# Spectral mixing and a snake feed-forward: from batch 2 on, one inverse matmul per spectrum class, with the halves of the spectrum swapped by DMA and the product added on VectorE

## The chip, the cores and the metric

The kernel runs on one core of one Trainium2 chip. The metric is the time of one execution in microseconds (us) of the device, taken as the median of several runs. The core has five engines, each working through its own list of instructions in order: TensorE (PE; its weight loads are shown apart as PEld), VectorE (DVE), ScalarE (ACT), GpSimd (POOL) and SyncE (SP). DMAs are issued from an engine's queue and run beside the engines.

## What is computed

The input has 8 batches (the code counts them 0 to 7; the second, number 1, is the first that changes) of 3008 positions and 256 channels.

```
X = rfft(x, axis=1)                    # x: (8, 3008, 256)
y = irfft(X * (filt_r + 1j * filt_i))  # global filter, per channel
h = y @ w_in                           # 256 -> 2048
g = h + sin(alpha * h)**2 / alpha
out = g @ w_out                        # 2048 -> 256
```

## The kernel before, in words

The transform of length 3008 = 47 x 64 is done as matrix products in three stages per batch. **Stage 1** (line 157, tile `pa`) makes 24 classes of the short transform and writes them to DRAM (`d1`). **Stage 2** reads them back with positions on the partitions (`t2`, line 169). For each class, one matmul with the table `d_t` (line 180, `pb`) gives 128 rows: 64 real parts and 64 imaginary parts. ScalarE copies the result of two classes to `xf` (line 183). VectorE multiplies `xf` by the filter's real part and by its imaginary part (line 187, two products `p`), and two accumulated matmuls per class (line 199, `pc`), with the table `e_t` and with a second one whose halves are exchanged and sign-changed, make the complex product and the inverse in one. The result is evacuated to `g` (lines 135 and 137, by ScalarE or VectorE in a rotation of three) and written to DRAM (`d2`, line 206). **Stage 3** loads `d2` as `t4` (line 214) and ends the inverse (line 219, `pd`), into the resident `y`.

The feed-forward part works on 48 chunks of up to 512 columns. For one block of 128 of the 2048 hidden channels, `hidden` does two matmuls (line 356, `ph`), a sine on ScalarE whose phase of pi/2 is read from the tile `quarter` (line 359, `cos`), and one VectorE instruction that forms the snake (line 360, `v`). `project` (line 371, `po`) multiplies the previous chunk's `v` by the second matrix; ScalarE copies the result (line 377) and SP stores it (line 389).

The order of work is a plan by **steps**, eight to a chunk: a step holds two blocks of `hidden` (four `ph` matmuls), whatever pieces of the stages are due, and eight `po` matmuls. `plan` (line 398) gives the due step of each piece of batch b, relative to step 48b: stage 1 at -45 to -38, stage 2 spread from -29 to about -16, stage 3 from -10 on. Batch 1 has its own due steps (line 407). Batch 0 is done ahead of the feed-forward part. A scheduler of the framework then fixes each engine's list and may move an instruction by some places; the pools set how far work may run ahead (PSUM: 4 buffers for `ph`, 2 shared by all stages' matmul results, 2 for `po`; `xf` has 3 buffers, `p` has 4).

The tables and the filter for the upper half of the partitions are made at the start (lines 267 to 292). POOL's queue carries the loads of `x` (line 118), the filters and the weights; SP's queue carries everything else.

Of the kernel before, what the change touches and what calls it, by code (L numbers as in the profile page):

```python
# [9 lines left out]
FP16 = mybir.dt.float16  # L10
FP32 = mybir.dt.float32
AFT = mybir.ActivationFunctionType
# [7 lines left out]
NS, NQ = 24, 64  # L20
NR = 2 * N1
NK = 4 * NS


def dft_tables():
# [29 lines left out]
def kernel(  # L55
# [28 lines left out]
    def pool(name, bufs, space=None):  # L84
        kw = {} if space is None else {"space": space}
        return ctx.enter_context(tc.tile_pool(name=name, bufs=bufs, **kw))
# [3 lines left out]
    t1pool = pool("t1", 4)  # L90
    t2pool = pool("t2", 4)
    xfpool = pool("xf", 3)
    ppool = pool("pp", 4)
    gpool = pool("gp", 4)
    t4pool = pool("t4", 3)
    opool = pool("op", 3)
# [8 lines left out]
    wf_t = cpool.tile([NR, NK], FP16)  # L105
    nc.sync.dma_start(out=wf_t, in_=wf_dram.ap())
    d_t = cpool.tile([128, NS, 128], FP16)
    e_t = cpool.tile([128, 2, NS, 128], FP16)
    wi_t = cpool.tile([NK, NR], FP16)
    f_t = [cpool.tile([128, NS, C], FP16, name=f"filt{i}") for i in range(2)]  # L110

    marks = {}

# [25 lines left out]
    def spectral(b):  # L139
# [8 lines left out]
        def stage1(u):  # L148
# [13 lines left out]
            if u == 7:  # L162
                st["t2"] = []
                for g in range(4):
# [5 lines left out]
                                          in_=d1[a0:a0 + 6, :, :].rearrange("s n c -> n s c"))  # L170
                    st["t2"].append(t2)

        def stage2(u):
            if u < 12:

                ps = (ops if b == 0 else fps).tile([128, 2, C], FP32, name=f"pb_{b}_{u}",
                                                   tag="o" if b == 0 else "f")
                for i in range(2):
                    s = 2 * u + i
                    nc.tensor.matmul(out=ps[:, i, :], lhsT=d_t[:, s, :],  # L180
                                     rhs=st["t2"][s // 6][:, s % 6, :], start=True, stop=True)
                xf = xfpool.tile([128, 2, C], FP16, name=f"xf_{b}_{u}", tag="xf")
                nc.scalar.copy(out=xf, in_=ps)  # L183
                pr = []
                for k in range(2):
                    pt = ppool.tile([128, 2, C], FP16, name=f"p_{b}_{u}_{k}", tag="p")
                    marks["prod", u] = nc.vector.tensor_tensor(out=pt, in0=xf, in1=f_t[k][:, 2 * u:2 * u + 2, :],  # L187
                                                               op=ALU.mult)
                    pr.append(pt)
                st["p", u] = pr  # L190
            if u > 0:
                w = u - 1
                pr = st.pop(("p", w))
                if w % 3 == 0:
                    st["g"] = gpool.tile([128, 6, C], FP16, name=f"g_{b}_{w}", tag="g")
                ps = fps.tile([128, 2, C], FP32, name=f"pc_{b}_{w}", tag="f")
                for i in range(2):
                    for k in range(2):
                        nc.tensor.matmul(out=ps[:, i, :], lhsT=e_t[:, k, 2 * w + i, :],  # L199
                                         rhs=pr[k][:, i, :], start=(k == 0), stop=(k == 1))  # L200
                i0 = 2 * (w % 3)
                evac(st["g"][:, i0:i0 + 2, :], ps, i0 != 2 if b == 0 else None)
                if w % 3 == 2:
                    for p in range(2):
                        a0 = p * NS + 6 * (w // 3)
                        nc.sync.dma_start(out=d2[a0:a0 + 6, :, :].rearrange("s n c -> n s c"),
                                          in_=st["g"][64 * p:64 * p + 64, :, :])

        def stage3(u):
            ch, rest = divmod(u, 4)  # L210
# [13 lines left out]

        for u in range(8):
            pieces.append((1, lambda u=u: stage1(u)))
        for u in range(13):
            pieces.append((2, lambda u=u: stage2(u)))
        for u in range(16):
            pieces.append((3, lambda u=u: stage3(u)))  # L230
        return pieces
# [6 lines left out]
    warm = cpool.tile([128, 1], FP32)  # L238
    nc.vector.memset(warm, 0.0)
    nc.scalar.activation(out=warm, in_=warm, func=AFT.Sin)  # L240
    quarter = cpool.tile([128, 1], FP32)
    nc.vector.memset(quarter, float(np.pi / 2))

    first = spectral(0)
    for _, piece in first[:8]:
# [20 lines left out]

    def dup_filter(g):
        gs = slice(6 * g, 6 * g + 6)
        for k in range(2):
            ins = nc.vector.tensor_copy(out=f_t[k][64:128, gs, :], in_=f_t[k][0:64, gs, :])  # L270
            behind(ins, marks["prod", 3 * g - 2] if g else s1_dve)

    for g in range(4):
        for k, filt in enumerate((filt_r, filt_i)):
            for q in range(2):
                off, step = ((6 * g) * C, C) if q == 0 else ((N1 - 6 * g) * C, -C)
                ins = nc.gpsimd.dma_start(
                    out=f_t[k][32 * q:32 * q + 32, 6 * g:6 * g + 6, :],
                    in_=bass.AP(tensor=filt.tensor, offset=filt.offset + off,
                                ap=[[N1 * C, 32], [step, 6], [1, C]]))  # L280
                if g >= 2:
                    after(ins, marks["t2", g - 2])
    for g in range(3):
        pse = ops.tile([128, 8, 128], FP16, name=f"pse_{g}", tag="o")
        for i in range(8):
            behind(nc.tensor.transpose(out=pse[:, i, :], in_=d_t[:, 8 * g + i, :], identity=id16),
                   s1_pe)
        gs = slice(8 * g, 8 * g + 8)
        behind(nc.scalar.mul(e_t[:, 0, gs, :], pse, 0.125), s1_act)
        nc.vector.tensor_copy(out=e_t[0:64, 1, gs, :], in_=e_t[64:128, 0, gs, :])  # L290
        nc.vector.tensor_scalar(out=e_t[64:128, 1, gs, :], in0=e_t[0:64, 0, gs, :],
                                scalar1=-1.0, scalar2=None, op0=ALU.mult)

    ones = cpool.tile([128, 128], FP32)
    nc.vector.memset(ones, 2.0)
# [53 lines left out]
    def hidden(k, jb):  # L349

        _, c0, n = chunks[k]
        if jb == 0:
            v[k] = vpool.tile([128, 16, 512], FP16, name=f"v_{k}", tag="v")
        ps = hps.tile([128, 512], FP32, name=f"ph_{k}_{jb}", tag="h")
        for cb in range(2):
            nc.tensor.matmul(out=ps[:, 0:n], lhsT=w1[:, cb, jb * 128:jb * 128 + 128],  # L356
                             rhs=y_cols[:, cb, c0:c0 + n], start=(cb == 0), stop=(cb == 1))
        cs = cospool.tile([128, 512], FP32, name=f"cos_{k}_{jb}", tag="c")
        nc.scalar.activation(out=cs[:, 0:n], in_=ps[:, 0:n], func=AFT.Sin, bias=quarter)  # L359
        marks["snake"] = nc.vector.scalar_tensor_tensor(  # L360
            out=v[k][:, jb, 0:n], in0=cs[:, 0:n], scalar=-1.0, in1=ps[:, 0:n],
            op0=ALU.add, op1=ALU.subtract)
# [18 lines left out]
    def store(o_blk, pb, col):  # L381

        p = 0
        while p < 128:
# [11 lines left out]


    plan = {1: [-45 + i for i in range(8)],
            2: [-29 + 14 * i / 13 for i in range(13)],
            3: [-10, -9] + [-7 + 2 * i for i in range(14)]}  # L400
    pending = [(1 + i % 4 + 8 * (i // 4), 0, piece) for i, (_, piece) in enumerate(first[25:])]
    for b in range(1, B):
        at = {1: 0, 2: 0, 3: 0}
        for stage, piece in spectral(b):
            at_step = 48 * b + plan[stage][at[stage]]
            if b == 1 and stage < 3:
                at_step = 8 + at[stage] if stage == 1 else 23 + at[stage]
            at[stage] += 1
            pending.append((at_step, b, piece))
    pending.sort(key=lambda p: p[0])  # L410
# [46 lines left out]
```

## Time and profile before

| what | us |
|---|---|
| median of 3 runs (839.6 to 840.46) | 840.31 |
| the profiled execution: its own time | 841.03 |
| its span, first to last instruction | 839.2 |
| what lies around the span (841.03 - 839.2) | 1.8 |
| TensorE matmuls (PE) busy | 799.2 |
| VectorE (DVE) busy | 628.4 |
| ScalarE (ACT) busy | 674.7 |
| GpSimd (POOL) busy | 28.3 |
| granted TensorE clock, mean over the span | 0.987 of full |

In the views of the profile, a line names an engine, a line of the kernel, the operation and the tiles as out<-in, with buffer numbers left out. The timeline gives the start of a group of equal instructions and how long the group took from the first start to the last end; neighbours on one engine overlap a little, so the pace is read from start to start. "Idle before" is the engine's idle time ahead of a group, with what ended it.

### The profile page before, as it was taken

To read this page: it belongs to the slowest core of one execution; us is meant where nothing else is said; L and a number is where in the kernel's file an instruction comes from. 1 tells how busy PE (TensorE), PEld (TensorE's weight loads), DVE (VectorE), ACT (ScalarE), POOL (GpSimd) and SP (SyncE) were. 2 spreads that over 40 slices of the span, in tenths; PEclk is the share of its full clock that TensorE was granted. 3 is DMA by queue.
4 is the path that set the end of the run, shared out by engine and by line. 5 is a ranking of instruction groups with operands and counts; after the bars stand their busy time and mean duration, and the time that the engine had idled before them with its cause. 6 is when DMAs were issued, how large, how long until landed. Compare 5 with 4: busy or idle time off the path is not lost.

```text
span 839.2 us, 16120 instructions
## 1 busy us (share of the span) xinstructions
PE 799.2 (95%) x5793; PEld 544.1 (65%) x5793; DVE 628.4 (75%) x1120; ACT 674.7 (80%) x1200; POOL 28.3 (3%) x55
## 2 busy tenths in 40 slices
PE   6748999999999999999999999999999999999996
PEld 2324676667776676666776677666767677666674
DVE  3658786777877787777877788777877778777772
ACT  4546897888878898888888888888988988788873
POOL 3210000000000000000000000000000000000000
PEclk9978999999999999999999999999999999999999
DMA  9985845184344734367242763447343343421111
GB/s 216 219 252 116 190 98 130 48 182 106 88 133 82 181 86 98 88 128 167 66 126 61 168 136 81 117 87 171 91 97 94 98 113 82 115 57 38 38 39 45
DMA packets 93495, 94.98 MB, mean 113 GB/s; under 512 B 8084, under 2 KB 82852, under 8 KB 93416
## 3 DMA queue, kind: packets, MB, share of 16 engines
q1 hardware_dynamic: 84784, 75.02, 34.4%
q0 software_dynamic: 6704, 18.09, 12.4%
q10 hardware_dynamic: 1928, 0.86, 0.5%
q8 instruction: 45, 0.74, 0.4%
q14 instruction: 34, 0.28, 0.1%
HBM read 58.02 MB, written 49.81 MB: 128 GB/s over the span
## 4 chain that ended last, share of the span: by engine, by line
PE 82%; DMA 7%; DVE 4%; ACT 4%; issue 2%; SPq 0%; POOL 0%; ACTq 0%; DVEq 0%; POOLq 0%
PE ph L356 35%; PE po L371 35%; PE pc L199 5%; PE pa L157 4%; PE pd L219 2%; DMA t<-d 2%; PE pb L180 2%; ACT cos L359 2%; DMA d<-t 1%; DMA w_out<-in_moe_w_out_dram 1%; DVE v L360 1%; DVE p L187 1%; DMA d<-g 1%; ACT t L135 1%; DMA filt<-in_filt_r_dram 1%
## 5 line engine op out<-in xcount | busy, mean ns | idle before, releaser
L360 DVE SCALAR_TENSOR_TENSOR v<-cos,ph 128x512 f16<-128x512 f32 (+1 forms) x768 | 483.8, 671 | 148.1 <-ACT cos L359 147.1
L359 ACT ACTIVATE cos<-ph,quarter 128x512 f32<-128x512 f32 (+1 forms) x768 | 480.6, 680 | 103.9 <-PE ph L356 101.6
L371 PE MATMUL po<-w,v 128*128 128x256 f16 x3008 | 401.3, 273 | 4.2 <-DVE w L339 4.2
L356 PE MATMUL ph<-y,w 128*128 128x512 f16 (+1 forms) x1536 | 391.3, 376 | 0.3 <-ACT y L135 0.2
L371 PEld LDWEIGHTS <-v 128*128 128x128 f16 x3008 | 289.0, 98 | 80.7 <-issue 8.9
L356 PEld LDWEIGHTS <-w 128*128 128x128 f16 x1536 | 150.6, 98 | 102.8 <-issue 5.5
L187 DVE TENSOR_TENSOR p<-xf,filt 128x512 f16<-128x512 f16 x192 | 72.1, 418 | 6.2 <-ACT xf L183 5.4
L377 ACT COPY o<-po 128x512 f32<-128x512 f32 x96 | 56.5, 589 | 9.8 <-PE po L371 7.4
L183 ACT CAST xf<-pb 128x512 f16<-128x512 f32 x96 | 56.6, 591 | 8.8 <-DMA t<-d 5.7
L135 ACT CAST t<-pa 96x512 f16<-96x512 f32 x89 | 50.0, 588 | 16.4 <-PE pa L157 16.4
L199 PE MATMUL pc<-p,e_t 128*128 128x256 f16 x384 | 59.9, 276 | 2.9 <-DVE p L187 1.5
L219 PEld LDWEIGHTS <-t 96*128 96x128 f16 x512 | 35.5, 98 | 39.0 <-DMA t<-d 11.8
L157 PE MATMUL pa<-x,wf_t 94*96 94x512 f16 x128 | 47.6, 410 | 9.7 <-DMA x<-in_x_dram 5.8
L219 PE MATMUL pd<-wi_t,t 96*128 96x94 f16 x512 | 42.3, 207 | 11.1 <-DMA t<-d 10.6
L135 ACT CAST y<-pd 128x376 f16<-128x376 f32 x82 | 38.7, 474 | 12.2 <-PE pd L219 12.2
L199 PEld LDWEIGHTS <-e_t 128*128 128x128 f16 x384 | 37.7, 99 | 15.7 <-issue 7.5
L180 PE MATMUL pb<-t,d_t 128*128 128x256 f16 x192 | 38.2, 283 | 3.5 <-DMA t<-d 2.4
L135 ACT CAST g<-pc 128x512 f16<-128x512 f32 x64 | 38.7, 605 | 2.2 <-PE pc L199 1.9
L137 DVE CAST y<-pd 128x376 f16<-128x376 f32 x46 | 25.2, 548 | 19.3 <-PE pd L219 19.1
L137 DVE CAST t<-pa 96x512 f16<-96x512 f32 x39 | 26.7, 684 | 16.8 <-PE pa L157 16.1
L180 PEld LDWEIGHTS <-d_t 128*128 128x128 f16 x192 | 18.7, 101 | 25.4 <-DMA t<-d 4.5
L118 POOL DMA_DIRECT2D x<-in_x_dram x32 | 16.6, 522 | 504.6 <-PE pa L157 494.0
(29 smaller groups left out, 86.1 us busy)
## 6 DMA issues: line engine op xcount, KB each, us to landing
d<-t SPq DMA_DIRECT2D x32, 384.0 KB
d<-g SPq DMA_DIRECT2D x64, 192.0 KB
t<-d SPq DMA_DIRECT2D x32, 384.0 KB
x<-in_x_dram POOLq DMA_DIRECT2D x32, 376.0 KB, 7.2
t<-d SPq DMA_DIRECT2D x60, 192.0 KB
out_dram<-o SPq DMA_DIRECT2D x72, 94.0 KB
w_in<-in_moe_w_in_dram POOLq DMA_DIRECT2D x2, 1024.0 KB, 9.0
w_out<-in_moe_w_out_dram POOLq DMA_DIRECT2D x1, 2048.0 KB, 12.4
```

What stands on the lines that cost most here:

```text
L135: marks["act"] = nc.scalar.copy(out=dst, in_=src)
L157: marks["pe"] = nc.tensor.matmul(out=ps[0:NK, :], lhsT=wf_t, rhs=st["x"][ch][:, n0:n0 + 2, :], start=True, stop=True)
L180: nc.tensor.matmul(out=ps[:, i, :], lhsT=d_t[:, s, :], rhs=st["t2"][s // 6][:, s % 6, :], start=True, stop=True)
L183: nc.scalar.copy(out=xf, in_=ps)
L187: marks["prod", u] = nc.vector.tensor_tensor(out=pt, in0=xf, in1=f_t[k][:, 2 * u:2 * u + 2, :], op=ALU.mult)
L199: nc.tensor.matmul(out=ps[:, i, :], lhsT=e_t[:, k, 2 * w + i, :], rhs=pr[k][:, i, :], start=(k == 0), stop=(k == 1))
L219: nc.tensor.matmul(out=psv[:, i, :], lhsT=st["t4"][:, 4 * half + i, cb * 128:cb * 128 + 128], rhs=wi_t, start=True, stop=True)
L356: nc.tensor.matmul(out=ps[:, 0:n], lhsT=w1[:, cb, jb * 128:jb * 128 + 128], rhs=y_cols[:, cb, c0:c0 + n], start=(cb == 0), stop=(cb == 1))
L359: nc.scalar.activation(out=cs[:, 0:n], in_=ps[:, 0:n], func=AFT.Sin, bias=quarter)
L360: marks["snake"] = nc.vector.scalar_tensor_tensor(out=v[k][:, jb, 0:n], in0=cs[:, 0:n], scalar=-1.0, in1=ps[:, 0:n], op0=ALU.add, op1=ALU. ...
L371: nc.tensor.matmul(out=pso[k][:, t % 2, :], lhsT=v[k][:, jb, 128 * t:128 * t + 128], rhs=w2[:, jb, :], start=(jb == 0), stop=(jb == 15))
L377: nc.scalar.copy(out=o[:, 0:nb, :], in_=pso[k][:, 0:nb, :])
```

## The change

Batch 0 keeps the old form (`stage2_first`), with the second table in three tiles of the pool `t4`. From batch 1 in the code's count, which is the second batch, a pair of classes u is worked on so:

- The forward matmuls and the copy to `xf` are as before. Two DMAs on POOL's queue, each of 64 partitions by 1 KB (64 KB), copy the lower half of `xf` to the upper half of a new tile `xs` and the upper half to the lower.
- VectorE multiplies `xf` by the filter's real part at once. Three steps later (`SWAP = 3`) it multiplies `xs` in place by the imaginary part, whose lower half now holds the negated values, and adds it to the first product: three VectorE instructions per pair where there were two.
- One step after that, one inverse matmul per class with `e_t` makes the result: two `pc` matmuls per pair where there were four.
- Stage 2 has 16 pieces in place of 13, at one per step from -30 to -15; for batch 1, from step 23 to 37 (before: 23 to 35).
- The sine takes its phase of pi/2 as a number in the instruction and not from a tile.

```diff
+SWAP = 3
-    ppool = pool("pp", 4)
+    ppool = pool("pp", 7)
+    xspool = pool("xs", 5)
...
         def stage2(u):
+
             if u < 12:
...
+                xf = forward(u)
+                xs = xspool.tile([128, 2, C], FP16, name=f"xs_{b}_{u}", tag="xs")
+                for p in range(2):
+                    nc.gpsimd.dma_start(out=xs[64 * p:64 * p + 64, :, :],
+                                        in_=xf[64 - 64 * p:128 - 64 * p, :, :])
+                st["p", u] = product(u, 0, xf), xs
+            w = u - SWAP
+            if 0 <= w < 12:
+                pt, xs = st["p", w]
+                nc.vector.tensor_tensor(out=xs, in0=xs, in1=f_t[1][:, 2 * w:2 * w + 2, :], op=ALU.mult)
+                nc.vector.tensor_tensor(out=pt, in0=pt, in1=xs, op=ALU.add)
+            w = u - SWAP - 1
+            if w >= 0:
+                inverse(w, [st.pop(("p", w))[0]])
...
-        for u in range(13):
-            pieces.append((2, lambda u=u: stage2(u)))
+        for u in range(13 if b == 0 else 13 + SWAP):
+            pieces.append((2, lambda u=u: (stage2_first if b == 0 else stage2)(u)))
...
-        nc.scalar.activation(out=cs[:, 0:n], in_=ps[:, 0:n], func=AFT.Sin, bias=quarter)
+        nc.scalar.activation(out=cs[:, 0:n], in_=ps[:, 0:n], func=AFT.Sin, bias=float(np.pi / 2))
...
-            2: [-29 + 14 * i / 13 for i in range(13)],
+            2: [-30 + i for i in range(13 + SWAP)],
...
-                at_step = 8 + at[stage] if stage == 1 else 23 + at[stage]
+                at_step = 8 + at[stage] if stage == 1 else 23 + 14 * at[stage] / 15
```

`forward`, `product` and `inverse` are the old lines of `stage2` cut into functions; `inverse` does one matmul per class for each product that it is given. At the start, the imaginary filter is loaded to the upper half of the partitions and its negated copy made for the lower half, and the second table of batch 0 is made by two sign changes in place of a copy and a sign change.

## The prediction

> **What bounds the kernel now.** First the page's busy times, then the slices, then the chain.
>
> ```profile
> PE 799.2 (95%) x5793; PEld 544.1 (65%) x5793; DVE 628.4 (75%) x1120; ACT 674.7 (80%) x1200; POOL 28.3 (3%) x55
> ...
> PE   6748999999999999999999999999999999999996
> ...
> PE 82%; DMA 7%; DVE 4%; ACT 4%; issue 2%; SPq 0%; POOL 0%; ACTq 0%; DVEq 0%; POOLq 0%
> ```
>
> TensorE is full from the fourth slice to the last but one, and the chain runs over it for 82% of the span. So the worth of a removed matmul is its own pace, as long as nothing else fills the hole. The windows view says what else is there: stage 2 of batch 3, and the stretch up to stage 2 of batch 4 (columns: us, then the busy time of PE, PEld, DVE, ACT, POOL).
>
> ```profile
> 291.31:327.82 36.51, 36.29 (x270) 25.96 (x268) 30.89 (x61) 31.77 (x57) 0.00 (x0) 1.00 0.40 90
> 327.82:390.10 62.28, 62.10 (x463) 41.94 (x461) 46.65 (x75) 52.47 (x94) 2.05 (x4) 1.00 0.55 129
> ```
>
> In stage 2 TensorE is busy for 36.29 of 36.51, but VectorE and ScalarE for some 31: only 5 to 6 us of cover each. The timeline gives the paces there.
>
> ```profile
> 301.86 0.75 DVE L187 TENSOR_TENSOR p<-xf,filt 128x512 f16<-128x512 f16 x2
> 302.53 0.68 DVE L137 CAST g<-pc 128x512 f16<-128x512 f32 x1
> 303.13 1.27 DVE L360 SCALAR_TENSOR_TENSOR v<-cos,ph 128x512 f16<-128x512 f32 x2
> 304.32 0.75 DVE L187 TENSOR_TENSOR p<-xf,filt 128x512 f16<-128x512 f16 x2
> ...
> 319.78 0.31 PEld L180 LDWEIGHTS <-d_t 128*128 128x128 f16 x2
> 320.00 0.38 PE L180 MATMUL pb<-t,d_t 128*128 128x256 f16 x2
> 320.22 0.60 PE L199 MATMUL pc<-p,e_t 128*128 128x256 f16 x4
> 320.65 1.04 PE L371 MATMUL po<-w,v 128*128 128x256 f16 x8
> 321.53 1.03 PE L356 MATMUL ph<-y,w 128*128 128x512 f16 x4
> ```
>
> From start to start: two `pb` 0.22, four `pc` 0.43, eight `po` 0.88, so 0.108 us per 256-column matmul. VectorE: two products 0.67 (0.335 each), a `g` evacuation 0.60, two snakes 1.19 (0.595 each). A plain step, `ph` and `po` alone, takes 1.74 (327.83 to 329.56 in the same timeline).
>
> **The removed matmuls.** Two per pair, 12 pairs, 7 batches: 168 x 0.108 = 18.1 us of TensorE. Their weight loads (99 ns in the group of line 199) lie under the matmuls and free nothing.
>
> **What VectorE then does to it.** I take the 17 steps from 291.31 to 329.56 of batch 3, 38.25 us. TensorE's work in them is 17 x 1.74 + 24 `pb` (2.6) + 48 `pc` (5.2) + one `pd` piece (0.17) = 37.5; 0.7 are short waits, mostly when VectorE does a `g`. After: 34.9. VectorE's own work rises from 34 x 0.595 + 24 x 0.335 + 4 x 0.60 = 30.7 to 34.7 (36 products and sums). So the two engines tie, and the load is uneven. By the built program's list for batch 3, eleven steps, from the fourth pair's on, hold 22 snakes, 28 products and sums and 4 evacuations: 13.1 + 9.4 + 2.4 = 24.9 us for VectorE, against 11 x 1.74 + 8 x 0.217 + 10 x 0.217 = 23.0 for TensorE. VectorE falls behind by 1.9. How much of that TensorE feels: a step's `ph` needs the snakes of two steps earlier (4 buffers), which leaves about 2 us, but an inverse matmul waits for its sum, and by the list it stands only 0.4 to 1 us behind it; behind the waiting `pc` stand all `po` and `ph`. I take 1.0 as absorbed, 0.9 as lost, and 0.3 of short waits kept: 34.9 + 0.9 + 0.3 = 36.1, a gain of 2.1 per batch. The ends are all lost (1.2) and nothing lost (3.3).
>
> **The swaps.** 168 DMAs of 64 KB on POOL's queue; the trace has none like them. The `x` loads stand ahead of the swaps in POOL's list, but wait only for stage 1 of the batch before, which is done 10 steps earlier, so they don't block. An `x` load on that queue occupies POOL for 0.51 us, moves its first packet 1.2 us after the start (at 264.5, 362.7, 557.5), and lands 0.3 after its last. With 4 packets per DMA engine at 0.05 to 0.07 us (the 1 KB stores), two swaps take 0.1 + 0.5 + 1.2 + 0.6 + 0.3 = 2.7 us from `xf` to landing, an estimate from these rows. The nearest whole rows are longer: filter loads of 96 KB at 27.7 to 31.6 took 4.6 to 5.4, the first of them with 2.9 us to its first packet beside `t2` loads; the `x` loads 4.6 to 8.3. I take 2.9, since outside the `t2` loads the DMA engines are 27 to 36% busy here, and keep 2.0 and 5.4 as the ends. VectorE's wait for a swap is in its list: behind it stand the snakes, and behind those ScalarE and `ph`. The plan leaves three steps (some 6 us), but the list puts the product of pair 0 in the very next step, and pair 3's too: about 2.7 us after `xf`. So 2.9 costs 0.2 to 0.4 once per batch, and the first pairs meet the tail of the `t2` loads, which run until 294.2 to 296.0 in batches 3 and 4 and to 492.3 in batch 5 (6.7 us into the window). I charge 0.5 per batch in all. At 5.4 it would be 2.5 more, at 2.0 nothing.
>
> The Trainium skill, DMA: Bandwidth & Descriptors, section "Anatomy of one DMA — SWDGE (gpsimd) path", gives about 2.0 us plus bytes/436e3 for such a DMA: 2.15 us for one swap, and 2.7 for two that start 0.5 apart. By that the first product would be on time and the 0.5 would be the `t2` tail alone.
>
> POOL's issues may be slower beside the products: the filter loads' at 27.7 to 31.6, among batch 0's products, took 0.49 to 0.78 us, at most 0.3 longer than the 0.51, which the three steps cover and the two early products pay at 0.3 each at worst.
>
> The Trainium skill, SBUF — State Buffer, section "SBUF: two separate sides", has a warning against this very queue: descriptors made by GpSimd are held up while VectorE runs in a two-port mode; the section "Who interferes with whom" takes products of two tensors out of that. By the warning every swap would come late, as in rival C; by the exception none.
>
> **Stage 3's start.** Stage 2 ends later: in the list the last `pc` stands two steps further on, with only 7.9 to 8.8 us of `po` and `ph` between it and the first `pd` (10.4 before). The chain in batch 3 was: `pc` ends 325.38, evacuated 326.34, two stores issued until 327.87, their packets end 331.1, `t4` issued 331.53, its packets end 334.1. That is 8.8. So 0 to 0.9 missing, 0.45 each, in batches 2 to 7: 2.7 us. In batch 1 the wait shows already:
>
> ```profile
> 143.43 0.33 SPq L214 DMA_DIRECT2D t<-d  x1
> 144.25 0.36 PEld L219 LDWEIGHTS <-t 96*128 96x128 f16 x8 [1.79 <-DMA t<-d]
> 144.26 0.51 PE L219 MATMUL pd<-wi_t,t 96*128 96x94 f16 x8 [1.51 <-DMA t<-d]
> ```
>
> There the chain took 10.75 (133.51 to 144.26). The list now fills it with 72 `po` (7.8 us), the whole of chunk 4's, and so has few left to mix into chunk 5, where TensorE will run at the pace of ScalarE and VectorE. I charge 1.5 more at the wait and 1.0 in chunk 5: 2.5, between 0 and 6.
>
> **The phase as a number.** `cos` takes 690 ns for 128x512, the same-sized copy of line 377 597 ns. Between 0 and 93 ns off 768 instructions, at most 71 us of ScalarE, which is not the bound: its cover is TensorE. It keeps ScalarE (busy 31.77 of 36.5 in stage 2) from becoming the bound in the shorter steps, and is worth up to 2 us where chunks 0 and 1 wait for it; I take 0.5. Cost elsewhere: none; the start-up's filter and table edits replace VectorE instructions one for one.
>
> **Sum.** 7 x (2.1 - 0.5) = 11.2; less 2.7, less 2.5, plus 0.5: 6.5 us off 841.03, so 834.5 by the profiled execution. The median shown is 0.7 lower; I forecast **834.0**.
>
> **Rivals.** (A) TensorE keeps all: VectorE's lag is absorbed and the swaps land in time. 7 x 3.3 = 23 less some 3 at stage 3: 820. For it, the 2 us of room at `ph`; against it, the tie of 34.9 and 34.7. Chance 0.12. (B) Gains and losses cancel within 0.2% (838.6 to 842.0): `pc` waits for its sum each time and all of the lag is lost, 7 x (1.2 - 0.5) - 2.7 - 2.5 + 0.5 = 0.2, so 840.1. For it, the sums that stand 0.4 us ahead of their `pc`; against it, the 2 us at `ph`. Chance 0.14. (C) Slower: swaps that land late. Each us beyond 2.9 delays VectorE once per batch at pair 0, by the list, and since VectorE has no idle time left the delay goes through to `pc`: 7 us per us. The 6.5 are used up at 3.8, and from 4.1 on it is slower by over 0.2%; at 5.4 it is 834 + 17.5 = 851.5. For it, the filter loads' 4.6 to 5.4; against it, that these read from DRAM beside full DMA engines. Chance 0.20. (D) That the change does not do what it says can be left out for the matmuls (the list has two per pair), and for the phase it would give back 0.5 and slow the lag's recovery; inside the range.
>
> The forecast's own case, 824 to 838.6, has 0.54. Faster by over 0.2% (about what a measurement of this kernel can tell from no change) is then 0.66, same 0.14, slower 0.20. The range, 820 to 848, leaves out about 0.2.
>
> **What would show it.** Line 199's successor with 216 matmuls; VectorE near 95% busy in the 17 steps and these 36 to 37 us long; two landings of a swap about 0.5 apart, the later some 2.9 us after its `xf`; waits of `pc` for the sum, short ones of the `xs` product for a DMA, and `pd` for `t4` of about 0.5 per batch and some 3 in batch 1; `cos` near 600 ns. Wrong it would be if the swaps took over 4 us, or if the 17 steps took over 38.

## The result, and the profile after

The change made the kernel slower: 862.11 us median (858.54 to 866.68, 4 runs) beside 840.38 for the kernel before in the same comparison, a ratio of 1.026 (1.020 to 1.031). The profiled execution took 860.53, with a span of 858.7 us and a granted clock of 0.983 (before: 0.987).

In the changed kernel's lines, `pb` is L186, `xf` L189, the first product L194, `pc` L204, the `d2` stores L211, the swaps L228, the product of the swapped half L234, the sum L235, the `t4` loads L245, `pd` L250, `ph` L388, `cos` L391, `v` L392, `po` L403 and the out stores L421. The page of the changed kernel: busy times, TensorE's slices, and the chain.

```profile
PE 787.1 (92%) x5625; PEld 523.7 (61%) x5625; DVE 650.5 (76%) x1203; ACT 617.1 (72%) x1200; POOL 115.8 (13%) x223
...
PE   6749988998999988999899989899899999899996
...
PE 64%; DMA 16%; DVE 8%; ACT 5%; issue 4%; SPq 1%; POOL 1%; ACTq 0%; DVEq 0%; POOLq 0%
```

The matmuls are gone as planned (5793 to 5625, 168 fewer), and TensorE is busy for 12 us less. But its row of nines now has eights all through, and the chain runs over DMAs for 16% of the span where it had 7%. TensorE lost more to waiting than it gained. The view of waits names the two new ones (us in total, times, longest).

```profile
PE pd L250 <- DMA t<-d: 23.4, 8, 8.6
...
DVE xs L234 <- DMA xs<-xf: 21.0, 10, 3.2
```

Before, `pd` waited for `t4` 10.6 us in 2 waits, 9.1 of them in batch 0; now it waits in every batch, 8.6 us in batch 0 and 14.8 in the other seven. The wait of VectorE for a swap is new: 21.0 us over 10 waits, one or two in each of seven batches.

To place the loss, I cut both spans at the first `ph` of a step, and measure the 17 steps that hold stage 2, the 8 steps after them up to the `pd` pieces, and the rest of each batch.

| stretch, us | before | after | difference |
|---|---|---|---|
| start to step 22 | 101.0 | 99.3 | -1.8 |
| batch 1: stage 2, 17 steps | 38.4 | 38.3 | -0.1 |
| batch 1: start of stage 3, 3 steps | 8.0 | 14.4 | +6.4 |
| batch 1: the 23 steps behind that | 45.9 | 41.1 | -4.8 |
| batches 2 to 7: stage 2, 17 steps each | 230.4 | 233.8 | +3.4 |
| batches 2 to 7: the 8 steps up to `pd` | 85.6 | 101.7 | +16.0 |
| batches 2 to 7: rest | 329.9 | 330.1 | +0.3 |
| span | 839.2 | 858.7 | +19.5 |

So there are two losses. Stage 2, which has 24 matmuls fewer in each batch, became no shorter. And the start of stage 3 costs 16 us more.

**Loss one, at the head of stage 2.** The timeline of batch 3 (start, duration, engine, what; in brackets the idle time before, with what ended it).

```profile
294.35 0.59 ACT L189 CAST xf<-pb 128x512 f16<-128x512 f32 x1
...
295.23 1.06 POOL L228 DMA_DIRECT2D xs<-xf  x2 [15.22 <-ACT xf L189]
...
300.48 0.42 DVE L234 TENSOR_TENSOR xs<-xs,filt 128x512 f16<-128x512 f16 x1 [2.75 <-DMA xs<-xf]
...
302.02 1.19 PE L388 MATMUL ph<-y,w 128*128 128x512 f16 x4 [1.11 <-DVE v L392]
...
302.64 1.19 ACT L391 ACTIVATE cos<-ph 128x512 f32<-128x512 f32 x2 [1.54 <-PE ph L388]
```

`xf` is done at 294.94 and POOL starts 0.29 us later, but the swapped halves are there only at 300.45, 5.5 us after `xf`. VectorE stands 2.75 us, the snakes queued behind it are late, and TensorE's `ph` waits for them. A second, later wait of TensorE (1.61 us, `pc` at 309.8) belongs to the same disturbance: in experiments 1 and 2 no such wait is left. From `xf` to both halves landed, pair 0 took 5.6, 5.6, 5.5, 5.1, 6.3, 4.3 and 5.0 us in batches 1 to 7; pairs 4 and 5, with few packets of SP's queue beside them, took mostly 2.6 to 3.3.

**Loss two, at the start of stage 3.** The timeline of batch 3 in the kernel before: SP's queue and `pd`.

```profile
326.61 1.26 SPq L206 DMA_DIRECT2D d<-g  x2
331.53 0.32 SPq L214 DMA_DIRECT2D t<-d  x1
332.11 1.89 SPq L389 DMA_DIRECT2D out_dram<-o  x5
334.04 0.78 SPq L214 DMA_DIRECT2D t<-d  x2
335.64 0.33 PE L219 MATMUL pd<-wi_t,t 96*128 96x94 f16 x4
```

The same in the changed kernel.

```profile
331.55 1.97 SPq L211 DMA_DIRECT2D d<-g  x2
...
333.83 2.16 SPq L421 DMA_DIRECT2D out_dram<-o  x5
...
336.46 1.25 SPq L245 DMA_DIRECT2D t<-d  x3
...
342.47 0.81 PE L250 MATMUL pd<-wi_t,t 96*128 96x94 f16 x8 [3.10 <-DMA t<-d]
...
344.56 1.06 PE L388 MATMUL ph<-y,w 128*128 128x512 f16 x2
```

Before, the first `t4` load was issued alone, and five out stores and the other two loads behind it. Now five out stores go ahead of it, and three loads are issued back to back. `pd` comes 6.0 us after the first load's issue; before, it came after 4.1 and did not wait. Besides, stage 2 ends nearer to `pd`: between the end of the last `pc` and `pd`, TensorE has 7.9 to 8.8 us of other work (the cover) in batches 2 to 7 (10.3 before), while the chain of evacuation, stores and load takes 9.1 to 11.9.

In this batch the wait of 3.10 us cost 5.0. The windows view shows why (columns as in the prediction; the clock is the third from the end).

```profile
339.40:342.40 3.00, 0.00 (x0) 0.00 (x0) 1.28 (x2) 0.54 (x2) 0.00 (x0) 0.97 0.90 255
342.40:344.00 1.60, 1.53 (x13) 1.29 (x14) 0.55 (x1) 0.47 (x1) 0.00 (x0) 0.50 0.10 38
344.00:346.00 2.00, 2.00 (x10) 1.12 (x9) 0.00 (x0) 0.58 (x1) 0.00 (x0) 0.60 0.00 0
346.00:348.00 2.00, 2.00 (x18) 1.28 (x16) 1.11 (x2) 1.63 (x4) 0.00 (x0) 1.00 0.37 107
```

With the wait TensorE's granted clock fell to half for 3.4 us, and its matmuls took twice as long: some 1.7 us on top.

### The profile page after: what moved, and what is told of

It reads as the page before. It is cut to its first block, busy times and chain, and to the rows that moved or that the text cites. A ratio compares the mean times of both kernels' runs of the same rounds, so it can differ in the third digit from the quotient of the medians.

```text
span 858.7 us, 16160 instructions
## 1 busy us (share of the span) xinstructions
PE 787.1 (92%) x5625; PEld 523.7 (61%) x5625; DVE 650.5 (76%) x1203; ACT 617.1 (72%) x1200; POOL 115.8 (13%) x223
## 4 chain that ended last, share of the span: by engine, by line
PE 64%; DMA 16%; DVE 8%; ACT 5%; issue 4%; SPq 1%; POOL 1%; ACTq 0%; DVEq 0%; POOLq 0%
PE ph L388 28%; PE po L403 28%; DMA t<-d 6%; DMA xs<-xf 5%; PE pa L164 3%; DVE v L392 3%; PE pc L204 2%; DMA d<-g 2%; PE pd L250 2%; ACT cos L391 2%; DMA d<-t 2%; DVE p L194 2%; DMA w_out<-in_moe_w_out_dram 1%; ACT t L142 1%; DVE xs L234 1%
## 5 line engine op out<-in xcount | busy, mean ns | idle before, releaser
L392 DVE SCALAR_TENSOR_TENSOR v<-cos,ph 128x512 f16<-128x512 f32 (+1 forms) x768 | 485.1, 671 | 133.9 <-ACT cos L391 133.2
L391 ACT ACTIVATE cos<-ph 128x512 f32<-128x512 f32 (+1 forms) x768 | 415.8, 591 | 141.0 <-PE ph L388 138.1
L403 PE MATMUL po<-w,v 128*128 128x256 f16 x3008 | 405.9, 273 | 2.5 <-DVE w L371 2.5
L388 PE MATMUL ph<-y,w 128*128 128x512 f16 (+1 forms) x1536 | 397.8, 377 | 7.7 <-DVE v L392 7.0
L403 PEld LDWEIGHTS <-v 128*128 128x128 f16 x3008 | 290.0, 98 | 82.4 <-issue 8.7
L388 PEld LDWEIGHTS <-w 128*128 128x128 f16 x1536 | 150.2, 98 | 106.7 <-issue 15.2
L228 POOL DMA_DIRECT2D xs<-xf x168 | 87.2, 524 | 270.5 <-ACT xf L189 266.4
L250 PEld LDWEIGHTS <-t 96*128 96x128 f16 x512 | 35.8, 101 | 52.8 <-DMA t<-d 26.7
L189 ACT CAST xf<-pb 128x512 f16<-128x512 f32 x96 | 57.4, 599 | 11.9 <-DMA t<-d 5.1
L250 PE MATMUL pd<-wi_t,t 96*128 96x94 f16 x512 | 43.5, 210 | 24.0 <-DMA t<-d 23.4
L142 ACT CAST t<-pa 96x512 f16<-96x512 f32 x89 | 51.1, 589 | 18.8 <-PE pa L164 18.7
L204 PE MATMUL pc<-p,e_t 128*128 128x256 f16 x192 | 39.9, 280 | 14.3 <-DVE g L144 8.5
L234 DVE TENSOR_TENSOR xs<-xs,filt 128x512 f16<-128x512 f16 x84 | 34.5, 419 | 21.0 <-DMA xs<-xf 21.0
L194 DVE TENSOR_TENSOR p<-xf,filt 128x512 f16<-128x512 f16 x108 | 43.9, 419 | 5.7 <-ACT xf L189 5.4
L142 ACT CAST g<-pc 128x512 f16<-128x512 f32 x64 | 38.0, 593 | 12.0 <-PE pc L204 11.2
L186 PE MATMUL pb<-t,d_t 128*128 128x256 f16 x192 | 37.8, 280 | 3.7 <-DMA t<-d 2.8
L204 PEld LDWEIGHTS <-e_t 128*128 128x128 f16 x192 | 14.6, 99 | 34.3 <-DVE p L235 16.4
```

The lines of the kernel that those rows point to most:

```text
L142: marks["act"] = nc.scalar.copy(out=dst, in_=src)
L194: marks["prod", u] = nc.vector.tensor_tensor(out=pt, in0=x, in1=f_t[k][:, 2 * u:2 * u + 2, :], op=ALU.mult)
L204: nc.tensor.matmul(out=ps[:, i, :], lhsT=e_of(k, 2 * w + i), rhs=pt[:, i, :], start=(k == 0), stop=(k == len(pr) - 1))
L228: nc.gpsimd.dma_start(out=xs[64 * p:64 * p + 64, :, :], in_=xf[64 - 64 * p:128 - 64 * p, :, :])
L250: nc.tensor.matmul(out=psv[:, i, :], lhsT=st["t4"][:, 4 * half + i, cb * 128:cb * 128 + 128], rhs=wi_t, start=True, stop=True)
L392: marks["snake"] = nc.vector.scalar_tensor_tensor(out=v[k][:, jb, 0:n], in0=cs[:, 0:n], scalar=-1.0, in1=ps[:, 0:n], op0=ALU.add, op1=ALU. ...
```

## The experiments

**1. No swaps.** The product reads `xf` itself; there are enough `xf` buffers, and `xs` is made by the product.

```diff
-                for p in range(2):
-                    nc.gpsimd.dma_start(out=xs[64 * p:64 * p + 64, :, :],
-                                        in_=xf[64 - 64 * p:128 - 64 * p, :, :])
...
-                nc.vector.tensor_tensor(out=xs, in0=xs, in1=f_t[1][...], op=ALU.mult)
+                nc.vector.tensor_tensor(out=xs, in0=xf_w, in1=f_t[1][...], op=ALU.mult)
```

> The changed kernel without its 168 swap DMAs: the product with the imaginary part reads the unswapped spectrum itself, so the exchange of the halves is left out of what is computed. Instructions on TensorE, VectorE and ScalarE are as many as in the changed kernel. Theory (late swaps): VectorE's idle 2 to 3 us ahead of the first such product of a batch goes, the 17 steps of stage 2 fall from a mean of 39.0 us by about 2 to 36.5 to 37.3, and seven batches give 13 to 16 us: 846 to 849 where the changed kernel takes 862. The start of stage 3 stays as long as it is (16 us over batches 2 to 7 more than before the change). Rival (VectorE bound by its 84 further instructions): the 17 steps stay at 38 to 39, and the time stays over 857. Rival (the swaps' traffic is what makes stage 3 late): the eight steps up to the first pd shrink by 2 to 3 us per batch as well, and the time is below 840.

Measured: 841.39 (838.12 to 844.09, 10 runs), ratio to the kernel before 0.999 (0.996 to 1.001). The 17 steps have a mean of 35.8 us over batches 2 to 7 (changed kernel 39.0, before 38.4), VectorE has no idle time ahead of these products, and the eight steps up to `pd` stay long: 100.7 in all (101.7 in the changed kernel). It came out below the 846 to 849 expected, since the 17 steps fell by 3.2 where I had put 2. VectorE's 84 further instructions do not hold the stage up, and the swaps' traffic is not what makes stage 3 late. Both rivals fall.

**2. The product where the plan means it.** `behind` puts an instruction behind another one in its engine's list.

```diff
+                if u < 12:
+                    behind(ins, marks["prod", u])   # ins: the product of xs of pair w = u - 3
```

> The changed kernel, with the product of pair u's swapped spectrum put behind the first product of pair u+3 in VectorE's list, three steps later, where the plan means it to be; the swaps are as before. Theory (late swaps met too early by VectorE's list): no idle time of VectorE ahead of these products is left, though the swaps still take 4 to 6 us; the 17 steps fall to 36.5 to 37.5 us and the time to 847 to 852. Rival (VectorE bound by its further instructions): the 17 steps stay at 38 to 39 and the time within 4 us of 862. Rival (the sum now stands too close ahead of its inverse matmul): the wait moves from VectorE to pc, the 17 steps get no shorter.

Measured: 845.28 (840.21 to 850.53, 10 runs), ratio 1.005 (1.003 to 1.008). The swaps take as long as before (pair 0: 4.5 to 6.0 us), but nobody waits. The same place in batch 3 of this kernel:

```profile
292.95 1.07 POOL L228 DMA_DIRECT2D xs<-xf  x2 [15.22 <-ACT xf L189]
...
299.40 0.42 DVE L234 TENSOR_TENSOR xs<-xs,filt 128x512 f16<-128x512 f16 x1
...
300.34 0.39 PE L204 MATMUL pc<-p,e_t 128*128 128x256 f16 x2 [0.20 <-DVE p L237]
```

And the 17 steps of batch 3 (us, then PE, PEld, DVE, ACT, POOL), first of the changed kernel:

```profile
290.84:329.33 38.49, 35.76 (x261) 24.30 (x259) 34.76 (x74) 30.07 (x59) 12.45 (x24) 1.00 0.61 137
```

then of this one:

```profile
288.56:324.20 35.64, 35.36 (x258) 23.86 (x256) 33.83 (x72) 30.12 (x59) 12.46 (x24) 1.00 0.64 146
```

TensorE is busy for 35.36 of 35.64 us and VectorE for 33.83: the tie holds without loss. The mean of the 17 steps is 35.8, as without swaps. So loss one was the place of the product in VectorE's list together with the swaps' 4 to 6 us, and it is worth 3.2 us per batch. What is left against the kernel before is stage 3's start (+18.7 in batches 2 to 7).

**3. The first `t4` load apart from the second.** `after` makes an instruction wait for the end of another one, here for the landing of the first load.

```diff
+                if b > 0 and ch == 1:
+                    after(ins, marks["t4"])   # ins: the second t4 load
```

> The changed kernel, with the second t4 load of each batch from batch 1 on issued only when the first has landed, so that the first has the DMA engines to itself; the engines' lists are the same. Theory (three loads issued back to back share the engines, so the first lands in 6 us and not in 2.6): it lands in about 3 us, the wait of pd falls by 2 to 3 us in each of batches 2 to 7, and the time falls by 10 to 16 us to 846 to 852. Rival (the chain is long because stage 2 ends later, whatever the loads do): the first load's time falls, but the time stays within 3 us of 862, or the wait moves to the second load's matmuls four steps later.

Measured: 856.86 (855.94 to 860.79, 4 runs), ratio 1.019 (1.016 to 1.022). The median is some 5 us below the changed kernel's where 10 to 16 were expected, and the spreads of the two overlap; the eight steps up to `pd` fell from 101.7 to 98.5. From the first load's issue to a `pd` that waits for it, it takes 3.6, 3.5 and 4.6 us in batches 2, 4 and 6 (4.2, 4.6, 5.4 in the changed kernel), and 5.4, 5.1 and 4.4 in batches 3, 5 and 7 (6.0, 5.9, 6.4), which have five out stores right ahead of it and not four. So the loads that follow it are one part of what slows the first. That the stores ahead of it are the other is not shown by this run, in which batch 7 with five of them took less than batch 6 with four.

**4. Stage 3 three steps later, in the even batches.**

```diff
+            if stage == 3 and b % 2 == 0:
+                at_step += 3
```

> The changed kernel, with stage 3 of batches 2, 4 and 6 due three steps later; the odd batches as they were, since their y is needed sooner, so they are the contrast inside the kernel. Theory (the start of stage 3 is a chain of 10 to 12 us that is no longer covered): in batches 2, 4 and 6 the wait of pd goes, and with it the 1.5 to 2.5 us that each of them loses in the eight steps up to pd; in all 4 to 6 us, 856 to 858, and nothing in batches 3, 5 and 7. Rival (work is only moved: TensorE or VectorE is short of time there anyway): the time stays within 2 us of 862, since what is gained at pd is lost where the pd pieces now stand closer together.

Measured: 863.56 (859.29 to 865.92, 4 runs), ratio 1.025 (1.022 to 1.029). The first half held: in batches 2, 4 and 6 the wait of `pd` is gone, and the eight steps take 13.9 us each (15.6 to 16.3 in the changed kernel). But the 17 steps of stage 2 in batches 2, 3 and 5 grew by 1.9, 2.5 and 0.8, the eight steps of batch 5 by 2.0, and the time did not fall. Part of this is the clock: the granted clock was at half for 3.4 us in batch 2's 17 steps (mean 0.96) and in batch 5's eight (mean 0.91), which costs 1.7 us each, and in neither of the two in the changed kernel (mean 1.00). In batches 3, 5 and 7, `pb` waits 1.7, 1.4 and 1.4 us for a `t2` load (1.0 in batch 5 of the changed kernel, and no such wait in 3 and 7); the `pd` pieces of the batch before, now later, may be what delays these loads, which no run shows. The time is the rival's, but only a part of the gain at `pd` was moved to other places; the clock took another part.

**5. The first `t4` load ahead of the out stores** (from experiment 2). It is issued with the last `d2` stores, and the out stores are put behind it in SP's list.

```diff
+            if b > 0 and w == 11:
+                load_t4(0)          # at the end of inverse(11)
...
+            behind(ins, marks["t4"])    # ins: an out store
```

> The kernel with the late product (845.28), and with the first t4 load of each batch put right behind the last d2 stores in SP's list, ahead of the out stores that now stand between them and ahead of the other t4 loads. Theory (the first load shares the DMA engines with four or five out stores and two further t4 loads, and so lands in some 6 us where it took 2.6): it lands in about 3 us, pd finds it about 8 us after the last pc, where the cover is 7.6 to 7.8 us by the list, the waits of 1.5 to 3.3 us fall under 0.6, and the time is 829 to 835. Rival (only the shrunken cover counts): the load gets shorter by less than 1 us, and the time stays over 840.

Measured: 830.83 (828.55 to 834.18, 4 runs), ratio 0.987 (0.984 to 0.990). Batch 3:

```profile
323.13 1.76 SPq L211 DMA_DIRECT2D d<-g  x2
327.19 0.32 SPq L218 DMA_DIRECT2D t<-d  x1
327.61 1.99 SPq L427 DMA_DIRECT2D out_dram<-o  x5
329.65 0.32 SPq L218 DMA_DIRECT2D t<-d  x1
330.76 0.34 PE L256 MATMUL pd<-wi_t,t 96*128 96x94 f16 x4 [0.67 <-DMA t<-d]
```

From issue to `pd` 3.3 to 3.7 us in all batches, and waits of 0.1 to 1.3. The cover is even shorter here than in the changed kernel (7.6 to 7.9 us), and still the eight steps come down from 104.3 to 90.9 us. Of these 13.4, about 10.5 are waits of `pd` (13.6 in experiment 2, 3.1 here), and 3.4 are the clock, which was at half for 3.4 us in batches 3 and 5 of experiment 2 and nowhere in these steps here. So most of loss two was the order of SP's list.

**6. Stages 1 and 2 three steps earlier** (from experiment 2).

```diff
-    plan = {1: [-45 + i for i in range(8)],
-            2: [-30 + i for i in range(13 + SWAP)],
+    plan = {1: [-48 + i for i in range(8)],
+            2: [-33 + i for i in range(13 + SWAP)],
```

> The kernel with the late product (845.28), with stages 1 and 2 of batches 2 to 7 due three steps earlier, so that 10.9 to 11.4 us of po and ph stand between the last pc and the first pd by TensorE's list where it had 7.9 to 8.6. Theory (the start of stage 3 is the rest of the loss, and is a matter of cover): with a chain of 9.5 to 11.8 us the waits fall from 1.5 to 3.3 us to under 0.9, the eight steps up to pd come back to 14 to 15 us from 15.8 to 19.3, and the time is 827 to 833. Rival (the work is only moved and collides with stage 3 of the batch before): the rest of each batch grows by what pd gains, and the time stays within 4 us of 845.

Measured: 828.33 (826.69 to 829.16, 4 runs), ratio 0.983 (0.982 to 0.985). The eight steps take 85.3 us, as before the change (85.6), and no `pd` waits from batch 2 on. The rest of the batches grew by 2.7, since stage 2 now begins two steps ahead of the 17, so little of the gain is given back. TensorE now has 10.7 to 11.2 us of other work between the last `pc` and `pd`. So more cover alone cures loss two as well.

**7. All three together:** the late product, the early load and the earlier plan.

> Late product, first t4 load ahead of the out stores, and stages 1 and 2 three steps earlier, all together. Theory: a chain of about 8 us under a cover of 10.9 to 11.4, so no wait for t4 from batch 2 on; what is left against the kernel before is batch 1's wait of about 2 us. 826 to 830. If it is no faster than the better of the two parts, either part alone was enough to cover the chain. Rival (SP's list, held up by the early load, delays the out stores and through the three o buffers the copies on ScalarE): waits of the o copy for out stores, and a time over 832.

Measured: 827.10 (826.57 to 828.53, 4 runs), ratio 0.982 (0.981 to 0.984): this version beats both kernels, by 1.8% and 4.1%. It is within the spread of experiment 6, so the earlier plan is enough, and the early load adds nothing clear to it. The 17 steps of batch 3 and the eight behind them:

```profile
286.62:322.21 35.59, 35.48 (x258) 23.77 (x256) 35.32 (x75) 30.33 (x58) 11.41 (x22) 1.00 0.50 124
322.21:336.79 14.58, 14.57 (x110) 9.88 (x108) 10.71 (x18) 10.20 (x20) 0.00 (x0) 1.00 0.49 140
```

TensorE and VectorE are both full in stage 2, and TensorE behind it: in stage 2, the matmuls that the change took away are now time that is saved.

**8. The swaps from SP's queue** (the changed kernel, early product).

```diff
-                    nc.gpsimd.dma_start(out=xs[64 * p:64 * p + 64, :, :],
+                    nc.sync.dma_start(out=xs[64 * p:64 * p + 64, :, :],
```

> The changed kernel, with the swaps issued from SP's queue in place of POOL's; product and plan as in the changed kernel. Theory A (the swaps are slow because their queue's packets get small turns beside the other queue's loads): on the other queue two swaps land 2.5 to 3.5 us after xf, VectorE's wait at pair 0 falls under 1 us, and the time falls by 8 to 13 us to 849 to 854. Theory B (the DMA engines are busy with the t2 loads, whatever the queue): they land after 4 to 6 us as before, and the time stays within 4 us of 862. Rival C (in SP's list the swaps stand behind stores and loads that wait): swaps begin late, the first over 1 us after xf, and the time is over 866.

Measured: 863.26 (859.52 to 869.00, 4 runs), ratio 1.025 (1.019 to 1.030). The time is theory B's, but in batches 1 to 6 the first swap starts 1.8 to 3.7 us after `xf`, as rival C has it, and VectorE still waits 17.3 us. Two things were changed at once, the queue and the place of the swaps behind SP's loads and stores, so the time tells nothing of the queue. But from its issue to the product that waited for it, pair 0's swap took 3.5 to 5.8 us here, and 4.0 to 6.0 from issue to landing on POOL's queue: the other queue did not make it quick, and theory A falls.

**9. Stage 1 four steps earlier** (the changed kernel), so that the `t2` loads are done before the first swaps.

```diff
-    plan = {1: [-45 + i for i in range(8)],
+    plan = {1: [-49 + i for i in range(8)],
```

> The changed kernel, with stage 1 of batches 2 to 7 due four steps (some 7 us) earlier and nothing else moved: VectorE's list for stage 2 is the same, with the early products, but the t2 loads are done before the first swaps start. Theory (the first swaps take 4 to 6 us because they share the DMA engines with the tail of the t2 loads): pair 0's swaps land 2.6 to 3.5 us after xf, VectorE's wait ahead of the first product falls from 1.6 to 3.2 us to under 0.8, the 17 steps from 39.0 to about 37, and the time to 848 to 853. Rival (these swaps are slow by themselves on POOL's queue): they still land after 4 to 6 us, and the time stays within 4 us of 862.

Measured: 863.98 (862.03 to 866.17, 4 runs), ratio 1.027 (1.025 to 1.030). My theory of the `t2` tail falls in this form. Pair 0's swaps did shorten, to 3.1 to 3.9 us in batches 2, 4, 6 and 7, with waits under 1 us; in batches 3 and 5 they still took 5.1. And where pair 0 was in time, VectorE waited for pair 1 or 2 in its place (2.6, 1.7, 2.4, 0.9 us in batches 2, 4, 6, 7). In all, VectorE waited 17.3 us where it had waited 21.0. Something else slows them: in the trace, out stores lie around these swaps.

**10 and 11. The out stores around the first swaps left out**, with stage 1 as in experiment 9 and then with stage 1 as the change has it.

```diff
+        if step > 48 and (step + 31) % 48 < 8:
+            return                  # in store()
```

> Stage 1 of batches 2 to 7 four steps earlier (as in the kernel that took 863.98), and the out stores of the eight steps around the first swaps of each of these batches left out, so that a part of the output is not written. Theory (a swap is slow whenever packets of SP's queue, of either kind, share the DMA engines with it): with neither t2 loads nor out stores beside them, the swaps of pairs 0 to 2 land 2.6 to 3.2 us after xf in every one of these batches, VectorE waits less than 0.5 us ahead of their products, the 17 steps fall to 36 to 37 us, and the time to 844 to 852. Rival (the swaps of pairs close together queue behind each other on POOL): pairs 1 and 2 still take 4 to 6 us and are waited for.

> The changed kernel with the same out stores left out (a part of the output is not written), stage 1 where the change has it, so that the t2 loads are still beside the first swaps. Theory (t2 loads and out stores both delay the swaps): pair 0 still takes 4 to 5 us in the batches whose t2 loads run past xf, pairs 1 to 3 fall to 2.6 to 3.5, and the time lies between the changed kernel's 862 and the kernel without either, at 850 to 858. Rival (only the out stores delay them): all pairs at 2.6 to 3.2 us, and the same time as without either. Rival (only the t2 loads do): no change for pair 0 to 2.

Measured: 852.48 (848.40 to 855.66, 4 runs), ratio 1.013 (1.010 to 1.016), and 860.66 (859.43 to 864.94, 4 runs), ratio 1.022 (1.019 to 1.026). The stretch of the 17 steps over batches 2 to 7 tells it apart:

| beside the first swaps | 17 steps, six batches, us |
|---|---|
| `t2` loads and out stores (the change) | 233.8 |
| out stores alone (experiment 9; 3.4 of it the clock's) | 232.1 |
| `t2` loads alone (experiment 11) | 230.5 |
| neither (experiment 10) | 222.2 |
| both, but not waited for (experiment 2) | 214.8 |

In experiment 9 the granted clock was at half for 3.4 us in the 17 steps of batch 2 and again of batch 4 (mean 0.96 in both), 1.7 us each; in the other rows it was 1.00. Without that, the out stores alone stand at 228.7.

With neither, pairs 2 and 3 take 2.6 to 2.7 us in most batches, close behind each other as they are, so they do not queue up on POOL. Pair 0 still took 4.7 and 5.1 us in batches 3 and 5, where an out store of the steps ahead was issued 1.7 and 0.9 us before it; one issued 1.3 us before it in batch 6 left it at 3.2. With `t2` loads alone, pair 0 stays at 4.0 to 6.3. Either kind of traffic is enough to delay a swap: taking one away gained 3.3 us (experiment 11) and 5.1 (experiment 9, without the clock's part), and taking both away 11.6, by one profiled execution each.

There is a third kind. In experiment 10, 36 pairs have no packet of SP's queue beside them. Most of these take 2.6 to 2.9 us, but pair 1 of batch 2, pair 2 of batch 4 and pair 3 of batch 6 take 3.8, 4.1 and 4.0, and VectorE waits 0.9, 1.1 and 0.4 us for them. Beside each of the three runs one 16 KB packet of a queue that the profile calls instruction, for 1.1 to 1.2 us from 1.0 to 1.6 us after the first swap's issue. Five other pairs meet such a packet earlier in their time and take 2.7 to 3.0. Experiment 10's time is half a us over what was expected, 11's by 2.7.

**12. Batch 1 earlier as well** (from experiment 6).

```diff
-                at_step = 8 + at[stage] if stage == 1 else 23 + 14 * at[stage] / 15
+                at_step = 7 + at[stage] if stage == 1 else 20 + 14 * at[stage] / 15
```

> The kernel with the late product and stages 1 and 2 three steps earlier (828.33), with batch 1's two stages moved as well: its stage 1 one step, its stage 2 three steps earlier. Theory (batch 1's start of stage 3 still waits for t4 by 1.7 us, and TensorE has used up the chunk's po there): the three steps around it fall from 15.7 us to 13 to 14, the wait to under 1 us, and the time by 1 to 2.5 us to 826 to 827.5. Rival (its earlier stage 2 meets chunks 0 and 1, where ScalarE and VectorE set the pace): steps 0 to 22 and 22 to 39 grow by as much.

Measured: 831.38 (829.66 to 833.56, 4 runs), ratio 0.989 (0.986 to 0.991). The start of stage 3 fell from 15.7 to 8.7 us, but steps 0 to 22 grew from 46.0 to 52.6 and the 23 steps behind from 41.6 to 45.2. The time went the rival's way, but its mechanism is not what the trace shows: 4.3 of the 6.6 us are one wait of `pb` for a `t2` load, with the clock at half for 3.4 us behind it. Batch 1's wait cannot be had cheaper this way.

**13 and 14. The phase**: read from a tile in the kernel of experiment 6, and as a number alone in the kernel before.

```diff
+    quarter = cpool.tile([128, 1], FP32)
+    nc.vector.memset(quarter, float(np.pi / 2))
...
-        nc.scalar.activation(out=cs[:, 0:n], in_=ps[:, 0:n], func=AFT.Sin, bias=float(np.pi / 2))
+        nc.scalar.activation(out=cs[:, 0:n], in_=ps[:, 0:n], func=AFT.Sin, bias=quarter)
```

> The kernel with the late product and stages 1 and 2 three steps earlier (828.33), with the sine's phase read from a tile again, as before the change. Theory (ScalarE is not the bound, with 29 us of work in the 36 us of stage 2): cos goes from 591 back to about 680 ns, and the time rises by 0 to 2 us. Rival (in the shorter steps of stage 2 ScalarE, with 0.09 us more on 34 sines, some 32 us, is now level with TensorE and holds it up): the 17 steps grow from 35.6 to 36.5 or more, and the time by 6 us or more.

> The kernel before the change, with the sine's phase as a number in the instruction and nothing else changed. Theory (ScalarE is not the bound except in the first chunks): cos falls from 680 to about 590 ns, steps 0 to 22 get shorter by 0.5 to 1.5 us, and the time by 0.5 to 2 us: 840 to 841.5 beside 842. Rival (ScalarE's speed is felt in every stage): 835 or less.

Measured: 831.40 (830.74 to 831.66, 4 runs), 3.1 more than experiment 6, with `cos` at 683 ns (592 there); the 17 steps hardly move (35.8 and 35.7), batch 2's rest takes 1.6 of it. And 839.81 (838.17 to 842.14, 10 runs) beside 841.01, ratio 0.998 (0.997 to 1.000), with `cos` at 590. There the gain is at the edge of what these runs tell, and steps 0 to 22, where I expected it, took 1.1 more in the profiled execution. The phase as a number is worth 1 to 3 us, and ScalarE is the bound in neither kernel.

## Why the prediction was wrong

By the profiled executions the change cost 19.5 us where the sum gave a gain of 6.5: 26.0 us apart.

| step of the prediction | forecast | measured | off by |
|---|---|---|---|
| stage 2, seven batches | -11.2 | +3.3 | 14.5 |
| start of stage 3, batches 2 to 7 | +2.7 | +16.0 | 13.3 |
| batch 1's wait and chunk 5 | +2.5 | +1.6 | -0.9 |
| start, phase and rest | -0.5 | -1.5 | -1.0 |

**The matmuls and VectorE's lag: right, and too careful.** 0.108 us for each of 24 matmuls gave 2.6 a batch, and with the swaps out of the way the 17 steps are shorter by just that, 38.4 to 35.8 (experiments 1, 2). In batch 3 TensorE stands for only 0.3 of them, so the 0.9 us that I had put down to VectorE's lag are not lost. The 2.6 lies between my 2.1 and the 3.3 of rival A. With the waits for the swaps gone, the seven stages are shorter by 18.5 us in experiment 2, for the 18.1 of the matmuls.

**The swaps: the step that failed first.** "I take 2.9 ... and keep 2.0 and 5.4 as the ends", "I charge 0.5 per batch in all". Pair 0's swaps took 5.3 us in the mean of seven batches, and they cost 3.2 us per batch (39.0 in the changed kernel, 35.8 in experiment 2). The nearest whole rows, the filter and `x` loads with 4.6 to 8.3 us, were the right witness; I set them aside because the DMA engines are only 27 to 36% busy there on average. At the moment of the first swaps they are not: the tail of `t2` and ten or so out stores lie there, and either is enough. (The tail was read loosely: by the trace before, the `t2` packets end at 295.9 in batch 3 and at 394.2 in batch 4, not both between 294.2 and 296.0.) That VectorE's list asks for the product one step after `xf` was read rightly, and with it rival C: its mechanism is what happened, with 5.3 us near its end of 5.4. Its price, 851.5, lacked the second loss. Both signs of being wrong that the prediction named came: swaps over 4 us, and 17 steps over 38 (39.0).

The estimate from the Trainium skill, DMA: Bandwidth & Descriptors, 2.7 us for two swaps, is what most quiet swaps take here (2.6 to 2.9). The same page, section "Issuing engines are not separate DMA queues", says that DMAs issued from any engine run on the same DMA engines and interleave; the table of experiments 9 to 11 agrees with that, and it was the part to apply. The warning about POOL's queue beside VectorE, which the prediction weighs, did not show: POOL's issues of the swaps took 0.52 us each (0.54 at most), and quiet swaps landed in 2.6 to 2.9 us with VectorE at the same products.

**Stage 3's start: the second step that failed.** "So 0 to 0.9 missing, 0.45 each". The cover was right: 7.9 to 8.8 forecast, 7.9 to 8.8 measured. The chain was not: I took its 8.8 us (8.7 by its own rows) over from the trace before, as if its links stayed. They did not: with stage 2 ending later, SP's list put four or five out stores ahead of the first load and the other loads right behind it. The prediction reads the lists of TensorE, VectorE and POOL in the built program, and not SP's. The chain became 9.1 to 11.9 us, the waits 1.2 to 3.1. Experiment 5, which gives SP's list its old order, takes 13.4 of 18.7 us back with no more cover, 3.4 of them by the clock. A smaller part, that a wait can bring half the clock for 3.4 us afterwards, was not in the sum at all.

**Batch 1** cost 1.6 where I charged 2.5: the wait came (+6.4 on its three steps), but the 23 steps behind it got shorter by 4.8, and chunk 5 did not slow down (10.5 us for its eight steps, 12.9 before). That the sum came close here is luck: neither of its two terms has its measured size.

**The range**, 820 to 848, ended below the result, because rival C and the start of stage 3 were priced one at a time; they came together.

## What to carry to other kernels

A transfer that is short by itself is priced with what else is in flight in the few microseconds when it runs, not with the mean share of the DMA engines in the stage; and it is placed so far ahead of its use, in the list of the engine that waits, that a doubled time does no harm. When a stage ends later, follow the queue of every engine on the chain to the next stage anew, the DMA issuer's above all: the order of loads and stores there can change without any line of them being touched. Removed matmuls are worth their time only once no wait takes their place: the same change, with one dependency and three plan steps added (experiment 6), ran at 0.983 of the kernel before.

## What the runs showed of the hardware

- The granted TensorE clock fell to 0.50 for 3.4 us after some waits of `pd`: after 3.10 us in the changed kernel (batch 3), but not after 2.44 and 2.85 us (batches 5, 7). In experiment 2 it fell after 1.73, 2.70 and 3.26 us, and not after 2.69. So the length of the wait alone does not decide it. The four executions of the changed kernel, 858.54, 860.53, 863.68 and 866.68 us, had mean clocks of 0.987, 0.983, 0.976 and 0.974, so a part of their spread is probably the clock's. Experiment 7, with one such wait left, lies within 2 us.
- The Trainium skill, TensorE: Matmul & The Clock Gate, section "What's actually happening", gives half the clock after an idle window of about 3.4 us, with windows that run freely. The halves above last 3.4 us each, which agrees; a wait of 1.73 us, which one of them followed, is less than a whole idle window.
- Two swaps of 64 KB take 2.6 to 2.9 us from `xf` to landing, 3.2 at most, with no packet of SP's queue and no 16 KB instruction packet beside them (28 pairs of experiment 10), up to 4.1 us beside one such instruction packet, and up to 6.6 us beside SP's transfers in the changed kernel, although the DMA engines were busy for only 0.61 of the time in the 17 steps of its batch 3.
